# Routed attention into a mixture of experts on one core: the first head pair's loads, transposes, copies and idle products rearranged, and the score scale moved into the exponential

## The chip, the cores and the metric

The kernel runs on one core of a Trainium2 chip. The metric is device time in microseconds from the start to the end of one execution. Its engines are named as in the profile: PE is TensorE (PEld its weight loads), DVE is VectorE, ACT is ScalarE, POOL is GpSimd, SP is SyncE, which here only issues DMA. SP, ACT and POOL each have a queue in which they can issue DMA.

## The reference

Attention with 4 batches, 8 heads, 768 positions and head size 64, in which a query sees only the keys that fall to the same of 16 centroids; then a layer of 8 experts for the 3072 rows that come out. Cut to what matters:

```python
q_n, k_n, c_n = ...                        # rows divided by their norm
q_assign = np.argmax(np.einsum('bhsd,hcd->bhsc', q_n, c_n), axis=-1)
k_assign = np.argmax(np.einsum('bhsd,hcd->bhsc', k_n, c_n), axis=-1)
mask = q_assign[:, :, :, None] == k_assign[:, :, None, :]
scores = (1.0 / np.sqrt(D)) * np.matmul(q, k.transpose(0, 1, 3, 2))
scores = np.where(mask, scores, -1000000000.0)
attn = softmax(scores)                     # with 1e-9 added to the sum
x = (attn @ v)  as rows of 512: 3072 x 512
# experts: gate logits x @ w_gate, the best expert e of each row,
# y = gate * (relu(x @ w1[e]) @ w2[e])
```

## The kernel before

The attention goes through 16 pairs of heads (`g`). For each pair, q and k are loaded with positions on the 128 partitions, transposed on PE to `qk` (two heads of 64 on the partitions), multiplied with the normed centroids (`similar`), transposed back (`similar2`), and turned into one-hot rows (`assign`, `assign2`), which `put` transposes to `ohT`. A score tile is then the sum of two products in one PSUM tile: q times k, and one-hot times one-hot, scaled so that a pair of different clusters lies 2 to the 60th lower. Numbers at the left are the line numbers that the profile uses.

```python
# loads (L691, L696, L702, L704): q, k, v by SP, the small ones by ACT
702  nc.scalar.dma_start(out=csb, in_=centroids...)
704  nc.scalar.dma_start(out=wg_in, in_=moe_w_gate...)     # 512 pieces of 32 B
705  for f in (load_qk, load_v):
706      for g in range(2): f(g)                           # L691 q, k; L696 v
     # identity, then products of it with itself before there is data
711  ps = ps_m.tile([P, 512], F32, name="mps")             # pool ps_m: one buffer
712  for i in range(12):
713      nc.tensor.matmul(ps[:, 0:P], lhsT=ident, rhs=ident, start=True, stop=True)
     # POOL, in this order
718  nc.gpsimd.memset(wg, 0.0)                             # then one_row, L720, L721
724  nc.gpsimd.tensor_copy(wg[r, :, a, 0:E], wg_in[r])     # twice
727  nc.gpsimd.memset(ohs, 0.0)
731  nc.gpsimd.memset(t[:, 1, :], 0.0)                     # ohT, twice
     # norms of the centroids
737  nc.scalar.activation(csq, csb, AF.Square, accum_out=cs2)
739  nc.scalar.activation(cnrm, cs2, AF.Sqrt)
741  nc.scalar.activation(csq[:, 0:1], cnrm, AF.Exp)       # brings the table of Exp
     # L743 to L748: cinv from cnrm on DVE; L752: cn = csb * cinv, twice
754  nc.tensor.transpose(cps[:, 0:P], cn..., ident)        # cps is the mps buffer
757  nc.gpsimd.memset(cblk, 0.0)
760  nc.vector.tensor_copy(cblk[...], cview[...])          # twice

     def turn(g, piece):          # piece 0: 6 of q, 2 of k; piece 1: 4 of k
773      nc.tensor.transpose(ps[...], rows[g, "qk"[w]][:, j]..., ident)
         if piece == 0:
778          (g == 1)  nc.scalar.mul(flat[:, 0:S], ps[:, 0:S], D**-0.5)
780          (others)  nc.vector.tensor_scalar_mul(flat[:, 0:S], ps[:, 0:S], D**-0.5)
781          nc.scalar.copy(flat[:, S:1024], ps[:, S:1024])
         else:
783          nc.scalar.copy(flat[:, 1024 : 2 * S], ps[:, 0 : 2 * S - 1024])

790  # similar: four products, cblk with qk; L795: copy to simT on DVE
801  # similar2: three transposes; L803: copy to sim on ACT
809  nc.vector.tensor_reduce(mx, sim, axis=AX, op=ALU.max)               # assign
810  nc.vector.tensor_tensor(sim, sim, mx..., op=ALU.is_ge)
811  nc.gpsimd.tensor_tensor(sim, sim, first_c..., op=ALU.mult)
817  nc.vector.tensor_reduce(top, rank, axis=AX, op=ALU.max)             # assign2
821  nc.vector.tensor_tensor(ohs..., rank, top..., op=ALU.is_equal)      # twice
831  # put: six transposes of ohs; L836: copy to ohT[:, 0] on ACT
838  nc.vector.tensor_scalar(oh[..., 1, :], ps..., scalar1=BIG, scalar2=-BIG, ...)  # twice

858  # score(u): q times k, two products; L861: one-hots, two products
863  nc.scalar.activation(A[u], ps[:, :, 0:HS], AF.Exp)
866  # and L870: DVE adds A to the sums T; L878: attend, A times v
```

The order in which these stand on the engines is written out by hand. Turns of six score tiles follow each other; before turn 0 there are only preparations:

```python
if g == 0:
    at(-4, 0, turn, g, 0)
    at(-4, 1, turn, g, 1)
    at(-3, 0, similar, g)
    at(-3, 1, similar2, g)
elif g == 1:
    at(-2, 1, turn, g, 0)
    at(-2, 1, turn, g, 1)
    at(-1, 1, similar, g)
    at(0, 0, similar2, g)
...
at(n - 2, 0, assign, g)
at(n - 2, 0, assign2, g)
at(n - 1, 0, put, g)
```

The tiles `sps` (two PSUM banks each) have three buffers, which transposes, similarities and scores share.

Of the kernel before, what the change touches and what calls it, by code (L numbers as in the profile page):

```python
# [8 lines left out]
F32 = mybir.dt.float32  # L9
BF16 = mybir.dt.bfloat16  # L10
I32 = mybir.dt.int32
AX = mybir.AxisListType.X
AF = mybir.ActivationFunctionType
ALU = mybir.AluOpType
# [170 lines left out]
def kernel(  # L185
# [11 lines left out]
    nc = tc.nc  # L197
    B, H, S, D = q.shape
    C = centroids.shape[1]
    P = 128  # L200
    NQ = S // P
    HP = H // 2
    NG = B * HP
    HS = S // 2
    G = 4 * NQ
    N = B * S
    Dm = H * D
    E = moe_w_gate.shape[1]
    F = moe_w1.shape[2]
    DB = Dm // P  # L210
# [14 lines left out]
    consts = ctx.enter_context(tc.tile_pool(name="consts", bufs=1))  # L225
# [15 lines left out]
    ident = consts.tile([P, P], F32)  # L241
    ident_b = consts.tile([P, P], BF16)

    def iota(name, shape, pattern, base, mult):
        ti = consts.tile(shape, I32, name=name + "_i")
        tf = consts.tile(shape, F32, name=name)
        nc.gpsimd.iota(ti, pattern=pattern, base=base, channel_multiplier=mult)
        nc.gpsimd.tensor_copy(tf, ti)
        return tf
# [11 lines left out]
    ps_s = late.enter_context(tc.tile_pool(name="ps_s", bufs=3, space=PSUM))  # L261
    ps_o = late.enter_context(tc.tile_pool(name="ps_o", bufs=1, space=PSUM))
    ps_m = late.enter_context(tc.tile_pool(name="ps_m", bufs=1, space=PSUM))
# [4 lines left out]
    def wide():  # L268
        return pools["s"].tile([P, 2, 512], F32, name="sps")
# [248 lines left out]
    def cols_of(t, c0):  # L518
        return lambda j: t[:, c0 + j : c0 + j + 1]
# [126 lines left out]
    def indices(pool, ps, w, gi, si):  # L646
# [14 lines left out]
            n=[P] * n, rows=NF * P, e=e, gi=cols_of(g_idx1, sum(FT[:e])), si=cols_of(s_idx1, sum(FT[:e])), apart=True,  # L661
# [6 lines left out]
    with ExitStack() as actx:  # L668
# [11 lines left out]
        rows = {}  # L680
# [5 lines left out]
        def load_qk(g):  # L686
            b, hp = divmod(g, HP)
            for name, src in (("q", q), ("k", k)):
                t = rows[g, name] = ld.tile([P, NQ, 2, D], F32, name=name + "_in")
                for a in range(2):  # L690
                    nc.sync.dma_start(out=t[:, :, a, :], in_=src[b, 2 * hp + a].rearrange("(p j) d -> p j d", j=NQ))  # L691

        def load_v(g):
            b, hp = divmod(g, HP)
# [5 lines left out]

        csb = consts.tile([P, D], F32)
        nc.scalar.dma_start(out=csb, in_=centroids.rearrange("h c d -> (h c) d"))  # L702
        wg_in = consts.tile([P, DB, E], F32)
        nc.scalar.dma_start(out=wg_in, in_=moe_w_gate.rearrange("(a p) e -> p a e", p=P))  # L704
        for f in (load_qk, load_v):
            for g in range(2):
                f(g)
        make_identity(nc, ident)
        nc.vector.tensor_copy(ident_b, ident)

        ps = ps_m.tile([P, 512], F32, name="mps")
        for i in range(12):
            nc.tensor.matmul(ps[:, 0:P], lhsT=ident, rhs=ident, start=True, stop=True)
        first_c = iota("first_c", [P, C], [[-1, C]], C, 0)
        first_e = iota("first_e", [P, E], [[-1, E]], E, 0)

# [12 lines left out]
        for i in range(2):  # L729
            t = ohp.tile([P, 2, S], BF16, name=f"ohT{i}")  # L730
# [3 lines left out]

        csq = consts.tile([P, D], F32)
        cs2 = consts.tile([P, 1], F32)
        nc.scalar.activation(csq, csb, AF.Square, accum_out=cs2)
        cnrm = consts.tile([P, 1], F32)
        nc.scalar.activation(cnrm, cs2, AF.Sqrt)

# [9 lines left out]
        cn = consts.tile([P, 2, D], F32)  # L750
        for a in range(2):
            nc.vector.tensor_scalar(cn[:, a, :], csb, scalar1=cinv[:, 0:1], scalar2=None, op0=ALU.mult)  # L752
        cps = ps_m.tile([P, 512], F32, name="mps")
        nc.tensor.transpose(cps[:, 0:P], cn.rearrange("p a d -> p (a d)"), ident)

        cblk = consts.tile([P, HP, 2, C], F32)
        nc.gpsimd.memset(cblk, 0.0)
        cview = cps[:, 0:P].rearrange("p (g a c) -> p g a c", a=2, c=C)
        for a in range(2):
            nc.vector.tensor_copy(cblk[a * D : (a + 1) * D, :, a, :], cview[a * D : (a + 1) * D, :, a, :])  # L760


        qk, sims, ohT = {}, {}, {}

        def turn(g, piece):

            if piece == 0:
                qk[g] = qkp.tile([P, 2, S], F32, name="qk")
            ps = ps_s.tile([P, 2, 512], F32, name="sps").rearrange("p a c -> p (a c)")
            n = 4 if piece else 8  # L770
            for i in range(n):
                w, j = divmod(8 * piece + i, NQ)
                nc.tensor.transpose(ps[:, i * P : (i + 1) * P], rows[g, "qk"[w]][:, j].rearrange("p a d -> p (a d)"), ident)  # L773
            flat = qk[g].rearrange("p w s -> p (w s)")
            if piece == 0:

                if g == 1:
                    nc.scalar.mul(flat[:, 0:S], ps[:, 0:S], D**-0.5)
                else:
                    nc.vector.tensor_scalar_mul(flat[:, 0:S], ps[:, 0:S], D**-0.5)  # L780
                nc.scalar.copy(flat[:, S:1024], ps[:, S:1024])
            else:
                nc.scalar.copy(flat[:, 1024 : 2 * S], ps[:, 0 : 2 * S - 1024])

        def similar(g):

# [18 lines left out]
        def assign(g):  # L805

            sim = sims.pop(g)
            mx = asg.tile([P, G], F32, name="mx")
            nc.vector.tensor_reduce(mx, sim, axis=AX, op=ALU.max)
            nc.vector.tensor_tensor(sim, sim, mx.unsqueeze(2).to_broadcast([P, G, C]), op=ALU.is_ge)  # L810
            nc.gpsimd.tensor_tensor(sim, sim, first_c[:, None, :].to_broadcast([P, G, C]), op=ALU.mult)  # L811
            sims[g] = sim

        def assign2(g):
# [29 lines left out]
        A, T, O = {}, {}, {}  # L844
# [6 lines left out]
        def score(u):  # L851
            g, half, j = where(u)
            qs = slice(half * HS, (half + 1) * HS)
            ks = slice(j * P, (j + 1) * P)
            ps = ps_s.tile([P, 2, 512], F32, name="sps")
            for a in range(2):
                r = slice(a * D, (a + 1) * D)
                nc.tensor.matmul(ps[:, a, 0:HS], lhsT=qk[g][r, 1, ks], rhs=qk[g][r, 0, qs], start=True, stop=False)  # L858
            for a in range(2):
                r = slice(a * D, (a + 1) * D)  # L860
                nc.tensor.matmul(ps[:, a, 0:HS], lhsT=ohT[g][r, 1, ks], rhs=ohT[g][r, 0, qs], start=False, stop=True)  # L861
            A[u] = ap.tile([P, 2, HS], F32, name="A")
            nc.scalar.activation(A[u], ps[:, :, 0:HS], AF.Exp)  # L863
            if j == 1:
                T[g, half] = tp_.tile([P, 2, HS], F32, name="T", bufs=3)
                nc.vector.scalar_tensor_tensor(  # L866
                    T[g, half], in0=A[u - 1], scalar=1e-9 / P, in1=A[u], op0=ALU.add, op1=ALU.add
                )
            elif j > 1:
                nc.vector.tensor_tensor(T[g, half], T[g, half], A[u], op=ALU.add)  # L870
# [105 lines left out]
        def at(n, part, f, *a):  # L976
            jobs.setdefault((n, part), []).append((f, a))
# [7 lines left out]
        for g in range(NG):  # L985
            n = g * TG
            if g == 0:
                at(-4, 0, turn, g, 0)
                at(-4, 1, turn, g, 1)
                at(-3, 0, similar, g)  # L990
                at(-3, 1, similar2, g)
            elif g == 1:

                at(-2, 1, turn, g, 0)
                at(-2, 1, turn, g, 1)
                at(-1, 1, similar, g)
                at(0, 0, similar2, g)
            else:
                at(n - 3, 0, turn, g, 0)
                at(n - 3, 0, turn, g, 1)  # L1000
                at(n - 3, 1, similar, g)
                at(n - 2, 0, similar2, g)
# [3 lines that stand above are left out]
            at(n, 1, finish, g, 0)  # L1006
            at(n + 1, 1, finish, g, 1)
            if g < NG - 1:
                at(n + 2, 0, weigh, g)
                at(n + 2, 1, weigh2, g)  # L1010
                at(n + 2, 1, x_turn, g, 0)
                at(n + 3, 1, x_turn, g, 1)
                if g % HP == HP - 1:
                    at(n + 3, 0, gate, g // HP)
                    at(n + 3, 1, keep_rows, g // HP)
# [41 lines left out]
        n = (NG - HP) * TG  # L1057
# [11 lines left out]
        n = NG * TG  # L1069
# [34 lines left out]
    with tc.tile_pool(name="sm", bufs=1) as sm:  # L1104
# [20 lines left out]
        for part in parts:  # L1125
            n, over = part["n"], part["over"]
# [8 lines left out]
        for t0 in range(0, NT, TQ):  # L1135
# [10 lines left out]
            op=ALU.is_le,  # L1146
# [62 lines left out]
    g = groups[0]  # L1209
# [11 lines left out]
    for i, g in enumerate(groups):  # L1221

        if i + 1 < ng:
            n = groups[i + 1]
# [11 lines left out]
        n = groups[i + 2] if i + 2 < ng else None  # L1236
# [22 lines left out]
    with tc.If(more > 0):  # L1259
        nx = nc.values_load(xe[0:1, NX : NX + 1], min_val=0, max_val=NX)  # L1260
        general = nc.values_load(xe[0:1, NX + 1 : NX + 2], min_val=0, max_val=1)
        with tc.If(nx > XU):
            with ExitStack() as ectx:
# [3 lines left out]
                with tc.For_i(XU, nx, 1) as i:  # L1267
# [4 lines left out]
                    g = dict(  # L1272
                        n=[P], rows=N, w=(fetch1(ex, 0), fetch2(ex, 0)), gi=lambda j: gi[:, 0:1], si=lambda j: gi[:, 1:2], apart=False
                    )
# [36 lines left out]
```

## Time and profile before

| | before |
|---|---|
| time, median of 3 runs | 798.7 us (798.4 to 799.66) |
| span of the profiled run | 802.5 us |
| PE busy | 774.7 us, 97% |
| DVE busy | 484.0 us, 60% |
| ACT busy | 307.1 us, 38% |
| POOL busy | 110.1 us, 14% |
| moved by DMA | 81.75 MB |

A row of a busy time tells how long an engine had something to do, not whether somebody waited for it. A timeline row gives the start, the duration, the engine, the source line, what was written from what, and in square brackets how long the engine had stood idle and which instruction released it. A "q" behind an engine's name means its queue of DMA issues. In the timeline's counts a product of 4-byte numbers has two records. Matmuls' ends are modelled.

### The profile page before, as it was taken

Reading aid. Unit: us, or ns where it says so; the run is one execution under the profiler, and the core shown is the slowest. Engines: PE = TensorE matmul, PEld = TensorE weight load, DVE = VectorE, ACT = ScalarE, POOL = GpSimd, SP = SyncE. Lnnn points to the kernel's source line nnn. Section 1 sums busy time; section 2 is a strip of 40 time slices with the busy share of each in tenths; the row PEclk is TensorE's granted clock in tenths of the full one; section 3 lists DMA queues with packets and bytes.
Section 4 is the critical chain, followed back from the end, with each engine's and each line's share of the span. In section 5 each row is a group of like instructions: output and inputs, shape, how many; then the busy total and the mean of one; then the engine's idle time right before and its main releaser. Section 6 shows DMA issues by size and latency. Waiting matters only on the chain.

```text
span 802.5 us, 11975 instructions
## 1 busy us (share of the span) xinstructions
PE 774.7 (97%) x4813; PEld 505.5 (63%) x4813; DVE 484.0 (60%) x783; ACT 307.1 (38%) x479; POOL 110.1 (14%) x164
## 2 busy tenths in 40 slices
PE   6999999999999999999999899999999999999994
PEld 4545454545444544444575697989797969696861
DVE  3667667767667767787536336867484847471610
ACT  4554654554655554645510123232323232232120
POOL 2200000000000000022005423030303020101010
PEclk8999999999999999999999999999999999999998
DMA  9026420382231222201010347252525233241240
GB/s 217 2 60 238 91 60 24 117 269 60 60 98 45 57 60 60 99 2 40 1 70 37 102 150 267 105 171 105 191 105 175 105 111 154 67 178 57 99 148 17
DMA packets 76191, 81.75 MB, mean 102 GB/s; under 512 B 52831, under 2 KB 56927, under 8 KB 75616
## 3 DMA queue, kind: packets, MB, share of 16 engines
q1 hardware_dynamic: 70208, 60.82, 24.8%
q0 software_dynamic: 5248, 20.04, 7.6%
q8 instruction: 40, 0.66, 0.3%
q14 instruction: 23, 0.19, 0.1%
q10 hardware_dynamic: 672, 0.05, 0.1%
HBM read 68.26 MB, written 13.68 MB: 102 GB/s over the span
## 4 chain that ended last, share of the span: by engine, by line
PE 74%; issue 12%; DVE 7%; POOL 3%; ACT 2%; POOLq 0%; ACTq 0%; DVEq 0%
PE sps L858 15%; PE sps L475 14%; PE O L878 13%; PE sps L497 8%; PE sps L363 4%; PE sps L309 4%; PE sps L861 3%; DVE T L870 3%; PE mps L899 3%; PE sps L790 2%; PE sps L290 2%; PE sps L773 2%; POOL out_dram L327 1%; PE sps L944 1%; PE mps L912 1%
## 5 line engine op out<-in xcount | busy, mean ns | idle before, releaser
L863 ACT ACTIVATE A<-sps 128x768 f32<-128x768 f32 x192 | 153.2, 812 | 53.1 <-PE sps L861 51.9
L858 PE MATMUL sps<-qk 64*128 64x384 f32 x768 | 160.4, 496 | 0.1
L870 DVE TENSOR_TENSOR T<-T,A 128x768 f32<-128x768 f32 x128 | 122.7, 958 | 14.3 <-ACT lsT L905 0.5
L878 PE MATMUL O<-A,v_in 128*64 128x384 f32 x768 | 130.9, 490 | 0.0
L858 PEld LDWEIGHTS sps<-qk 64*128 64x128 f32 x768 | 66.9, 189 | 50.1 <-issue 42.5
L878 PEld LDWEIGHTS O<-A,v_in 128*64 128x64 f32 x768 | 52.3, 137 | 62.7 <-issue 62.6
L327 POOL DMA_INDIRECT out_dram<-zo,s_idx x34 | 33.0, 970 | 255.1 <-ACT zo L509 170.6
L363 PE MATMUL sps<-w,h_sb 128*128 128x512 f32 x144 | 63.6, 596 | 0.0
L861 PE MATMUL sps<-ohT 64*128 64x384 bf16 x384 | 63.6, 325 | 0.0
L866 DVE SCALAR_TENSOR_TENSOR T<-A 128x768 f32<-128x768 f32 x32 | 30.6, 958 | 49.3 <-ACT A L863 49.3
L475 PEld LDWEIGHTS sps<-xs,w1s 128*128 128x128 f32 x336 | 56.4, 190 | 5.7 <-issue 5.7
L475 PE MATMUL sps<-xs,w1s 128*128 128x208 f32 (+1 forms) x336 | 59.4, 333 | 0.6 <-DVE xs L385 0.6
L811 POOL TENSOR_TENSOR sim<-sim,first_c 128x384 f32<-128x384 f32 x16 | 16.0, 1000 | 263.8 <-DVE sim L810 263.8
L490 ACT ACTIVATE h_sb<-h_sb 128x832 f32<-128x832 f32 (+1 forms) x28 | 24.3, 867 | 69.8 <-DVE h_sb L431 69.8
L363 PEld LDWEIGHTS sps<-w,h_sb 128*128 128x128 f32 x144 | 26.7, 190 | 30.8 <-issue 30.6
L273 POOL DMA_INDIRECT xg<-x_rows,g_idx x34 | 36.6, 1078 | 38.5 <-ACT xgT L298 17.1
L497 PE MATMUL sps<-w2s,hs 128*128 128x256 f32 x168 | 38.6, 379 | 1.8 <-DVE w2s L385 1.8
L475 PE MATMUL sps<-xgT,w 128*128 128x208 f32 (+1 forms) x224 | 40.0, 331 | 0.0
L886 ACT COPY xT<-O 128x384 f32<-128x384 f32 x32 | 15.5, 484 | 61.6 <-PE O L878 61.6
L475 PEld LDWEIGHTS sps<-xgT,w 128*128 128x128 f32 x224 | 38.0, 190 | 0.0
L351 DVE TENSOR_TENSOR zc<-zc,sps 32x512 f32<-32x512 f32 x8 | 5.4, 675 | 53.6 <-ACT zc L350 53.6
L323 ACT ACTIVATE zo<-sps,gate 128x512 f32<-128x512 f32 x12 | 8.3, 688 | 73.9 <-PE sps L363 49.7
(246 smaller groups left out, 1063.0 us busy)
## 6 DMA issues: line engine op xcount, KB each, us to landing
w<-in_moe_w_dram SPq DMA_DIRECT2D x20, 2048.0 KB, 8.5
x_rows<-x POOLq DMA_DIRECT2D x4, 1548.0 KB
q_in<-in_q_dram SPq DMA_DIRECT2D x32, 192.0 KB, 4.5
k_in<-in_k_dram SPq DMA_DIRECT2D x32, 192.0 KB, 4.8
v_in<-in_v_dram SPq DMA_DIRECT2D x16, 384.0 KB, 3.3
xg<-x_rows,g_idx POOLq DMA_INDIRECT x34
out_dram<-zo,s_idx POOLq DMA_INDIRECT x34
csb<-in_centroids_dram ACTq DMA_DIRECT2D x1, 32.0 KB, 1.9
```

Source lines behind the costliest of these rows:

```text
L273: nc.gpsimd.indirect_dma_start(out=g["xg"][0:m, j, :], out_offset=None, in_=x_d[0 : g["rows"], :], in_offset=bass.IndirectOffsetOnAxis(ap= ...
L309: nc.tensor.matmul(o, lhsT=g["w"][0][:, c, fb * P : (fb + 1) * P], rhs=g["xT"][:, c, :cols], start=(c == 0), stop=(c == DB - 1),)
L327: ins = nc.gpsimd.indirect_dma_start(out=out[:, :], out_offset=bass.IndirectOffsetOnAxis(ap=g["si"](j)[0:m], axis=0), in_=zo[0:m], in_offs ...
L363: nc.tensor.matmul(zp, lhsT=g["h"][:, fb, j * P : (j + 1) * P], rhs=g["w"][1][:, fb, :], start=(fb == 0), stop=(fb == FB - 1),)
L475: nc.tensor.matmul(o, lhsT=a[:, c, f * P : (f + 1) * P], rhs=b[:, c, :], start=(c == 0), stop=(c == KH - 1),)
L497: nc.tensor.matmul(ps[:, 0, 0:DH], lhsT=a[:, f, :], rhs=b[:, f, :], start=(f == 0), stop=(f == FH - 1),)
L858: nc.tensor.matmul(ps[:, a, 0:HS], lhsT=qk[g][r, 1, ks], rhs=qk[g][r, 0, qs], start=True, stop=False)
L861: nc.tensor.matmul(ps[:, a, 0:HS], lhsT=ohT[g][r, 1, ks], rhs=ohT[g][r, 0, qs], start=False, stop=True)
L863: nc.scalar.activation(A[u], ps[:, :, 0:HS], AF.Exp)
L866: nc.vector.scalar_tensor_tensor(T[g, half], in0=A[u - 1], scalar=1e-9 / P, in1=A[u], op0=ALU.add, op1=ALU.add)
L870: nc.vector.tensor_tensor(T[g, half], T[g, half], A[u], op=ALU.add)
L878: nc.tensor.matmul(O[g, half][a * D : (a + 1) * D, 0:HS], lhsT=rows[g, "v"][:, a, j, :], rhs=a_[:, a, :], start=(j == 0), stop=(j == NQ - 1),)
```

## The change

The change concerns what happens before and while the first pair of heads is prepared, and, in two points, all pairs. Its parts:

- k of the first pair is issued by ACT's queue instead of SP's, so that q and k are issued side by side. The small load of `w_gate` goes from ahead of these loads to behind them.
- Squares and their sum for the centroids' norms move from ACT (with a table of its own) to DVE.
- The centroids' transpose and the copies to `cblk` go behind the first eight transposes of q and k, as a function `blocks`.
- A piece of `turn` now holds the same four positions of q and of k, so each fills one PSUM bank: DVE copies q's bank, ACT copies k's. The second piece (two positions of each) is copied by ACT.
- The scale 1/8 is no longer multiplied into q, but given to the exponential.
- The rank product of the first pair (L811) is done by DVE instead of POOL.
- The products of the identity with itself that keep PE busy ahead of the data are 8 instead of 12, and 3, 2 and 9 more stand in three gaps of the preparation.

```diff
-                    nc.sync.dma_start(out=t[:, :, a, :], in_=src[b, 2 * hp + a]...)
+                    (nc.scalar if g == 0 and name == "k" else nc.sync).dma_start(
+                        out=t[:, :, a, :], in_=src[b, 2 * hp + a]...)
 ...
         nc.scalar.dma_start(out=csb, in_=centroids...)
-        nc.scalar.dma_start(out=wg_in, in_=moe_w_gate...)
         for f in (load_qk, load_v):
             for g in range(2):
                 f(g)
+        nc.scalar.dma_start(out=wg_in, in_=moe_w_gate...)
 ...
+        def idle(ps, n):
+            for i in range(n):
+                nc.tensor.matmul(ps[:, 0:P], lhsT=ident, rhs=ident, start=True, stop=True)
+        def idle_of(n):
+            idle(ps_m.tile([P, 512], F32, name="mps"), n)
         ps = ps_m.tile([P, 512], F32, name="mps")
-        for i in range(12):
-            nc.tensor.matmul(ps[:, 0:P], lhsT=ident, rhs=ident, start=True, stop=True)
+        idle(ps, 8)
 ...
-        nc.scalar.activation(csq, csb, AF.Square, accum_out=cs2)
+        nc.vector.tensor_tensor(csq, csb, csb, op=ALU.mult)
+        nc.vector.reduce_sum(cs2, csq, axis=AX)
 ...     # cps, its transpose and the two copies to cblk: into a function
+        def blocks():
 ...
-            n = 4 if piece else 8
-            for i in range(n):
-                w, j = divmod(8 * piece + i, NQ)
-                nc.tensor.transpose(ps[...], rows[g, "qk"[w]][:, j]..., ident)
+            n = NQ - 4 if piece else 4
+            for i in range(2 * n):
+                w, j = divmod(i, n)
+                nc.tensor.transpose(ps[...], rows[g, "qk"[w]][:, 4 * piece + j]..., ident)
             if piece == 0:
-                if g == 1:
-                    nc.scalar.mul(flat[:, 0:S], ps[:, 0:S], D**-0.5)
-                else:
-                    nc.vector.tensor_scalar_mul(flat[:, 0:S], ps[:, 0:S], D**-0.5)
-                nc.scalar.copy(flat[:, S:1024], ps[:, S:1024])
+                nc.vector.tensor_copy(qk[g][:, 0, 0:512], ps[:, 0:512])
+                nc.scalar.copy(qk[g][:, 1, 0:512], ps[:, 512:1024])
             else:
-                nc.scalar.copy(flat[:, 1024 : 2 * S], ps[:, 0 : 2 * S - 1024])
+                nc.scalar.copy(qk[g][:, :, 512:S], ps[:, 0 : 2 * n * P]...)
 ...
-            nc.gpsimd.tensor_tensor(sim, sim, first_c..., op=ALU.mult)
+            (nc.gpsimd if g else nc.vector).tensor_tensor(sim, sim, first_c..., op=ALU.mult)
 ...
-            nc.scalar.activation(A[u], ps[:, :, 0:HS], AF.Exp)
+            nc.scalar.activation(A[u], ps[:, :, 0:HS], AF.Exp, scale=D**-0.5)
 ...
                 at(-4, 0, turn, g, 0)
+                at(-4, 0, blocks)
                 at(-4, 1, turn, g, 1)
+                at(-4, 1, idle_of, 3)
                 at(-3, 0, similar, g)
+                at(-3, 0, idle_of, 2)
                 at(-3, 1, similar2, g)
             elif g == 1:
                 at(-2, 1, turn, g, 0)
                 at(-2, 1, turn, g, 1)
+                at(-2, 1, idle_of, 9)
```

More of the change, by code (lines that the diff above doesn't have):

```diff
@@ L690, in load_qk @@
                 for a in range(2):
-                    nc.sync.dma_start(out=t[:, :, a, :], in_=src[b, 2 * hp + a].rearrange("(p j) d -> p j d", j=NQ))
+                    (nc.scalar if g == 0 and name == "k" else nc.sync).dma_start(
+                        out=t[:, :, a, :], in_=src[b, 2 * hp + a].rearrange("(p j) d -> p j d", j=NQ)
+                    )
         def load_v(g):
@@ L702 @@
         nc.scalar.dma_start(out=csb, in_=centroids.rearrange("h c d -> (h c) d"))
-        wg_in = consts.tile([P, DB, E], F32)
-        nc.scalar.dma_start(out=wg_in, in_=moe_w_gate.rearrange("(a p) e -> p a e", p=P))
         for f in (load_qk, load_v):
@@ L707 @@
                 f(g)
+        wg_in = consts.tile([P, DB, E], F32)
+        nc.scalar.dma_start(out=wg_in, in_=moe_w_gate.rearrange("(a p) e -> p a e", p=P))
         make_identity(nc, ident)
         nc.vector.tensor_copy(ident_b, ident)
+        def idle(ps, n):
[3 more added lines that the diff above has]
+            idle(ps_m.tile([P, 512], F32, name="mps"), n)
         ps = ps_m.tile([P, 512], F32, name="mps")
-        for i in range(12):
-            nc.tensor.matmul(ps[:, 0:P], lhsT=ident, rhs=ident, start=True, stop=True)
+        idle(ps, 8)
         first_c = iota("first_c", [P, C], [[-1, C]], C, 0)
@@ L752 @@
             nc.vector.tensor_scalar(cn[:, a, :], csb, scalar1=cinv[:, 0:1], scalar2=None, op0=ALU.mult)
-        cps = ps_m.tile([P, 512], F32, name="mps")
-        nc.tensor.transpose(cps[:, 0:P], cn.rearrange("p a d -> p (a d)"), ident)
         cblk = consts.tile([P, HP, 2, C], F32)
         nc.gpsimd.memset(cblk, 0.0)
-        cview = cps[:, 0:P].rearrange("p (g a c) -> p g a c", a=2, c=C)
-        for a in range(2):
-            nc.vector.tensor_copy(cblk[a * D : (a + 1) * D, :, a, :], cview[a * D : (a + 1) * D, :, a, :])
+        def blocks():
+            cps = ps_m.tile([P, 512], F32, name="mps")
+            nc.tensor.transpose(cps[:, 0:P], cn.rearrange("p a d -> p (a d)"), ident)
+            cview = cps[:, 0:P].rearrange("p (g a c) -> p g a c", a=2, c=C)
+            for a in range(2):
+                nc.vector.tensor_copy(cblk[a * D : (a + 1) * D, :, a, :], cview[a * D : (a + 1) * D, :, a, :])
         qk, sims, ohT = {}, {}, {}
@@ L768, in turn @@
                 qk[g] = qkp.tile([P, 2, S], F32, name="qk")
-            ps = ps_s.tile([P, 2, 512], F32, name="sps").rearrange("p a c -> p (a c)")
-            n = 4 if piece else 8
-            for i in range(n):
-                w, j = divmod(8 * piece + i, NQ)
-                nc.tensor.transpose(ps[:, i * P : (i + 1) * P], rows[g, "qk"[w]][:, j].rearrange("p a d -> p (a d)"), ident)
-            flat = qk[g].rearrange("p w s -> p (w s)")
-            if piece == 0:
-                if g == 1:
-                    nc.scalar.mul(flat[:, 0:S], ps[:, 0:S], D**-0.5)
-                else:
-                    nc.vector.tensor_scalar_mul(flat[:, 0:S], ps[:, 0:S], D**-0.5)
-                nc.scalar.copy(flat[:, S:1024], ps[:, S:1024])
+            n = NQ - 4 if piece else 4
+            ps = wide().rearrange("p a c -> p (a c)")
+            for i in range(2 * n):
+                w, j = divmod(i, n)
+                nc.tensor.transpose(ps[:, i * P : (i + 1) * P], rows[g, "qk"[w]][:, 4 * piece + j].rearrange("p a d -> p (a d)"), ident)
+            if piece == 0:
+                nc.vector.tensor_copy(qk[g][:, 0, 0:512], ps[:, 0:512])
+                nc.scalar.copy(qk[g][:, 1, 0:512], ps[:, 512:1024])
             else:
-                nc.scalar.copy(flat[:, 1024 : 2 * S], ps[:, 0 : 2 * S - 1024])
+                nc.scalar.copy(qk[g][:, :, 512:S], ps[:, 0 : 2 * n * P].rearrange("p (w s) -> p w s", w=2))
         def similar(g):
@@ L810, in assign @@
             nc.vector.tensor_tensor(sim, sim, mx.unsqueeze(2).to_broadcast([P, G, C]), op=ALU.is_ge)
-            nc.gpsimd.tensor_tensor(sim, sim, first_c[:, None, :].to_broadcast([P, G, C]), op=ALU.mult)
+            (nc.gpsimd if g else nc.vector).tensor_tensor(sim, sim, first_c[:, None, :].to_broadcast([P, G, C]), op=ALU.mult)
             sims[g] = sim
```

## The prediction

> **What bounds the kernel now.** I read the page first. It has TensorE (PE) busy for 774.7 of 802.5 us, 97% of the span, so an operation on another engine is worth nothing unless PE stands and waits for it. The two rows of forty slices (one slice is 20 us) tell where PE is not full: the first digit is 6, nearly all others are 9, and the granted clock is below full in the first slice too. The change works on that slice.
>
> ```profile
> PE   6999999999999999999999899999999999999994
> ...
> PEclk8999999999999999999999999999999999999998
> ```
>
> Then I read the timeline of the first 26 us for the order of events (columns: start, duration, engine, line, tiles; in square brackets what the engine waited for):
>
> ```profile
> 1.21 0.45 ACTq L704 DMA_DIRECT2D wg_in<-in_moe_w_gate_dram  x1
> 4.72 0.47 POOL L724 COPY wg<-wg_in 64x32 f32<-64x32 f32 x2 [2.20 <-DMA wg_in<-in_moe_w_gate_dram]
> 5.25 0.74 POOL L727 MEMSET oh<- 128x768 bf16 x1
> 5.92 1.50 POOL L731 MEMSET ohT<- 128x768 bf16 x2
> 7.37 0.20 POOL L757 MEMSET cblk<- 128x128 f32 x1
> 7.60 0.46 DVE L760 COPY cblk<-mps 64x64 f32<-64x64 f32 x2 [0.85 <-POOL cblk L757]
> 8.11 0.96 DVE L780 TENSOR_SCALAR qk<-sps 128x768 f32<-128x768 f32 x1
> 9.21 1.64 PE L790 MATMUL sps<-qk,cblk 128*32 128x384 f32 x8 [0.71 <-DVE qk L780]
> 13.84 0.99 POOL L811 TENSOR_TENSOR sim<-sim,first_c 128x384 f32<-128x384 f32 x1 [6.28 <-DVE sim L810]
> 16.14 0.82 PE L831 MATMUL sps<-ident_b,oh 128*128 128x128 bf16 x6 [2.77 <-DVE oh L821]
> 25.12 0.33 PE L861 MATMUL sps<-ohT 64*128 64x384 bf16 x2
> ```
>
> The rows form one chain: similarities of the first pair at 9.21, the transposes of its one-hot rows (L831) at 16.14, the last of the first six score tiles done at 25.12 + 0.33 = 25.45. From there PE is full. So **25.45 is the mark**: moving it moves the whole program, and nothing else in the change does. Note also what stands ahead of 9.21: GpSimd (POOL) waits for the small load wg_in until 4.72, then clears oh and the two ohT, and only then clears cblk, which VectorE (DVE) needs before it may write the centroid blocks. DVE lost 0.85 us to it already.
>
> Last, the clock by stretches (PE busy, clock, DMA share, GB/s):
>
> ```profile
> 8.55:11.95 3.40, 2.07 (x12) 1.00 1.14 299
> 11.95:15.35 3.40, 1.42 (x14) 1.00 1.33 235
> 15.35:18.75 3.40, 2.61 (x16) 0.54 1.23 265
> 18.75:22.15 3.40, 3.40 (x14) 0.50 0.52 84
> ```
>
> PE ran at half clock from about 15.6 to 22.2, after a stretch in which it was busy for 1.42 of 3.40 us.
>
> **What the Trainium skill says.** "TensorE: Matmul & The Clock Gate", part "What's actually happening": the clock is either half or full, and a free-running window of about 3.4 us decides it from how busy PE was. The trace agrees: 0.50 and 1.00 are the only levels, and the change back comes near 22.2 after a full stretch. That is the reason for the idle products. "DMA: Bandwidth & Descriptors", "Issuing engines are not separate DMA queues": two issuing engines share the same 16 DMA engines, only issue time is saved. "ScalarE: Activation LUTs", "What ACT_TABLE_LOAD costs": about 1283 ns a load; the trace has 1.28 us three times (1.69, 3.35, 4.87).
>
> **The change part by part.**
>
> 1. *Two queues.* In the old trace the four loads of the first pair were issued on one queue at 0.78, 1.51, 2.19 and 2.87 and landed 3.6, 3.9, 4.1 and 4.3 us later: 4.4, 5.4, 6.3, 7.2. About 0.9 us a load of 192 KB is 218 GB/s, the rate that the DMA view shows throughout: transfer sets the landings, not issue. With k on ScalarE's queue all four are in flight at once; the early slices, which had only 108 to 206 GB/s, fill up, so k lands perhaps 0.3 to 0.7 us sooner, but q, now sharing with k, later than 5.4.
>
> 2. *wg_in goes to the end of ScalarE's queue.* Issue starts after csb (ends 1.18) and two k loads of about 0.65 us each: 2.5. With its old 3.5 us to landing that is 6.0; behind 384 KB of k in the same queue I take **7.0** (between 6.0 and 7.8), against 4.7 now.
>
> 3. *What hangs on it.* POOL's order is unchanged, so from landing to a cleared cblk it is 7.57 - 4.72 = 2.85 us, and to the end of the two block copies on DVE 8.06 - 4.72 = 3.34 us: 7.0 + 3.34 = 10.35. Then the three idle products: they write the one mps buffer, which still holds the centroids' transpose, so they wait for the block copies and then stand ahead of the similarities. A product is two records; the warm ones at the end of L713 come eight in 0.9 us, 0.23 us a product, so 0.7 us. Similarities start at **11.1**, 1.9 us later than now.
>
> 4. *The other inputs are hidden behind that.* Loads by 7.0, eight transposes 1.0 (0.11 each and the tail), copy of 512 columns on DVE 0.96 - 256/0.96 ns = 0.69, then two copies on ScalarE (ACT) of 0.6 each: about 9.8. The two engines do not overlap here: in the built program's list of waits ACT's copy still waits for DVE's, as it did (ACT lost 2.7 us to DVE qk L780). So transposes ahead of the centroids' and the new banks gain nothing visible. The squares on DVE save a table load of 1.28 us, but the two k issues of 1.3 us now stand in front of ACT's first table load; the root comes at about 4.5 instead of 4.64. Zero.
>
> 5. *Similarities to one-hots.* Now 16.14 - 9.21 = 6.93 us. The eight records took 1.64 us because the second half waited for ACT; with all inputs ready later pairs take 0.85: -0.8. The rank product moves from POOL (0.99 plus a hand-over) to DVE, where its sister L810 takes 0.56: 13.84 to 14.87 becomes about 0.6, -0.45. Left 5.7. Beside it PE has the two idle products, three transposes, twelve of pair 1 (1.5 us) and nine idle products (2.1 us): done about 5.4 after the start if warm, so just in time. One-hot transposes at 11.1 + 5.7 = **16.8**, 0.65 later than now.
>
> 6. *Scores at full clock.* From L831 to the mark it is now 25.45 - 16.14 = 9.31 us. Warm: transposes until ACT can start 0.55 (0.86 cold), copy of ohT 0.80, two mask operations 1.14, hand-overs 0.3, last ohT product 0.33, then five tiles of 0.81 (the steady distance of L858) = 4.05: 7.15. That is -2.15.
>
> 7. *The scale in the exponential and the split copies in later pairs.* An Exp takes 0.81 us with or without it. In later pairs DVE's copy loses 0.27 us and ACT's gain 0.23, in series as before; PE waited for these copies about 4 us in all (2.4 for ACT L781, 1.6 for DVE qk). I put 0, within 0.5.
>
> Sum: +1.9 - 0.8 - 0.45 - 2.15 = -1.5 us at the mark.
>
> **Rivals.**
> (a) *The load of wg_in hides nothing* because two queues carry far more than one, and it lands near 6.0: similarities at 10.1, mark 2.5 us earlier, about 796.2. For it: between 3.5 and 4.0, with both queues active, 263 GB/s flowed. Against it: 217 GB/s in most other slices.
> (b) *The gap before the blocks makes the clock fall.* PE has nothing between the end of the transposes (about 8) and the idle products (10.4). In the stretch 8.55 to 11.95 it would be busy for about 1.5 us, like the 1.42 that cost the clock before. Then the nine idle products run at 0.43 us and hold up the one-hots by 1 to 2 us: gain 0, about 798.7. If also the first six tiles stay cold, 2.15 is not won and the kernel is up to 0.7 us slower. I give this 35%. The eight products at the start, which end near 4.9 instead of about 6.1, could also fail to raise the clock at all.
> (c) *Nothing waits for wg_in*, and the author's order pays in full: blocks at 8.5, similarities at 9.3, mark 3.3 us earlier, 795.4. The list of waits speaks against it.
>
> **Range and chances.** From 798.7: -1.5 by the sum, with a third of weight on (b), gives -1.3, 797.4 us. The best reading of (a) with some luck in later pairs is 795.8; the worst of (b) with half a microsecond of noise (runs before lie 798.4 to 799.66) is 799.3. The whole opening is 25 us and 2% is 16 us, so within 2% is all but certain.
>
> **What would show it right or wrong.** Right: POOL's copy of wg starts between 6 and 7.8; DVE's block copies have an idle time "POOL cblk" of over 1 us ahead of them; similarities start between 10 and 12, after the idle products; the rank product is 0.56 on DVE; clock 1.00 at the first scores; last of six tiles near 24. Wrong: wg_in landing before 5.5, PE waiting for ACT's copies of qk rather than for the blocks, a clock of 0.50 at the scores, or waits at L790 of later pairs that differ by over 1 us in sum. A time under 795 or over 800 would mean that something outside the opening moved.

## The result and the profile after

The changed kernel takes 803.06 us (802.52 to 803.37, 4 runs) against 799.18 us for the kernel before (798.4 to 800.13): ratio 1.0047, interval 1.003 to 1.0065. It is 3.9 us slower, where 1.3 us faster was predicted, and lies above the stated range of 795.8 to 799.3 us, though well within 2%.

First the timeline of the changed kernel, the rows that answer to those shown of before (start, duration, engine, line, what; in brackets the idle time and who ended it):

```profile
2.58 0.67 ACTq L710 DMA_DIRECT2D wg_in<-in_moe_w_gate_dram  x1
...
6.50 1.09 PE L785 MATMUL sps<-ident,q_in 128*128 128x128 f32 x4 [1.31 <-DMA q_in<-in_q_dram]
...
8.52 0.69 DVE L787 COPY qk<-sps 128x512 f32<-128x512 f32 x1 [2.14 <-PE sps L785]
...
8.70 0.47 POOL L733 COPY wg<-wg_in 64x32 f32<-64x32 f32 x2 [6.19 <-DMA wg_in<-in_moe_w_gate_dram]
...
9.25 0.58 ACT L788 COPY qk<-sps 128x512 f32<-128x512 f32 x1 [2.96 <-DVE qk L787]
...
11.26 0.20 POOL L764 MEMSET cblk<- 128x128 f32 x1
11.49 0.46 DVE L772 COPY cblk<-mps 64x64 f32<-64x64 f32 x2 [2.28 <-POOL cblk L764]
...
12.09 1.62 PE L716 MATMUL mps<-ident 128*128 128x128 f32 x6 [2.54 <-DVE cblk L772]
...
13.64 1.51 PE L797 MATMUL sps<-qk,cblk 128*32 128x384 f32 x8
...
20.54 0.51 PE L838 MATMUL sps<-ident_b,oh 128*128 128x128 bf16 x6
...
28.10 0.39 PE L868 MATMUL sps<-ohT 64*128 64x384 bf16 x2
```

Read down the starts. POOL waits 6.19 us for wg_in and gets it at 8.70, where it was 4.72. It clears oh and the two ohT, then cblk at 11.26. DVE has stood idle 2.28 us for that; the three idle products have waited for DVE's copies and take 1.62 us before the similarities may start at 13.64 (9.21 before). The mark, the end of the first six score tiles, is 28.10 + 0.39 = 28.49 us. Note also ACT's first copy of qk: 2.96 us idle, released by DVE's copy. The "two engines from two banks" work one after the other.

The opening of the kernel before is itself not fixed. A second profile of it, described below, has its mark at 23.87 us instead of 25.45 and no loss near 460 us, where the first one lost 3.4 us. Its 799.43 us lies in the middle of 28 timed runs of the kernel before (median 799.56), so the fair comparison is 28.49 against 23.87. From the mark to the end, the second profile of before needs 797.6 - 23.87 = 773.7 us, the changed kernel 801.6 - 28.49 = 773.1. Together 4.6 - 0.6 = 4.0 us: the 3.9 us that were timed. **All of the loss, and slightly more, is in the first 28 us.**

### The profile page after: what moved, and what is told of

It is laid out like the page before. It is cut to its first block, busy times and chain, and to the rows that moved or that the text cites. A ratio compares the mean times of both kernels' runs of the same rounds, so it can differ in the third digit from the quotient of the medians.

```text
span 801.6 us, 12011 instructions
## 1 busy us (share of the span) xinstructions
PE 776.4 (97%) x4833; PEld 508.3 (63%) x4833; DVE 481.7 (60%) x787; ACT 308.6 (39%) x475; POOL 109.3 (14%) x163
## 4 chain that ended last, share of the span: by engine, by line
PE 74%; issue 12%; DVE 6%; POOL 3%; ACT 2%; DMA 1%; ACTq 0%; POOLq 0%; DVEq 0%
PE sps L865 14%; PE sps L475 14%; PE O L885 13%; PE sps L497 8%; PE sps L363 4%; PE sps L309 4%; PE sps L868 3%; PE mps L906 3%; DVE T L877 3%; PE sps L797 2%; PE sps L290 2%; PE sps L785 1%; POOL out_dram L327 1%; PE sps L951 1%; ACT A L870 1%
```

## The experiments

The variants ran on several chips, whose level for the kernel before differs by 2 us (medians 799.5 to 801.6); only ratios, each to the kernel before on the same chip, are compared. On one of these chips (the variants cblk_pair1, after_one_queue, before_idle_rank and before_idle_rank_split) the profiles also show about 3.5 us lost near 460 us, as the first profile of before does, so these four spans are not set against the others'; their openings are.

### The kernel before, once more (before_again)

No edit.

> The kernel before, unchanged, for a second profile. In its first profile the first six score tiles ended at 25.45 us and some 3.6 us were lost near 460 us, and that execution was about 5 us over the median of the timed ones. Theory A (the changed kernel is slower because its opening is longer): the opening is the same again, mark near 25.4, and what was lost near 460 us is not there. Rival B (the clock's window falls differently in each execution): the half clock from 15.6 to 22.2 us is missing in this execution, and the mark lies near 23.3.

Measured: 799.43 us, mark 23.87. The half clock was there, but shorter. Windows of this second profile (PE busy, clock, DMA share, GB/s):

```profile
15.30:18.70 3.40, 2.77 (x18) 0.65 1.24 263
18.70:22.10 3.40, 3.40 (x26) 0.85 0.50 81
```

In the first profile the clock was at half from 15.6 until 22.4 (the prediction read 22.2; the column has 0.58 between 22.0 and 22.5); here it is at half from 16.3 to 19.7. Neither expectation held fully: the clock fell in both, but for 3.4 us in one and for 6.8, twice as long, in the other. The Trainium skill, "TensorE: Matmul & The Clock Gate", part "What's actually happening", calls the window free-running, and these two executions agree with it. My mark of 25.45 was the long one.

### wg_in issued ahead of k (after_wg_first)

```diff
+        wg_in = ...; nc.scalar.dma_start(out=wg_in, ...)
         for f in (load_qk, load_v): ...
-        wg_in = ...; nc.scalar.dma_start(out=wg_in, ...)
```

> The changed kernel with one thing undone: the load of wg_in is issued ahead of k's loads again. Theory A (wg_in's landing at 8.70 us holds up GpSimd's clearing of cblk, so the similarities start at 13.64): landing near 4.9, block copies right behind DVE's copy of qk at about 9.2, similarities near 11.1, mark (end of the first six score tiles) 2.5 us earlier than the changed kernel's 28.49, time about 800.5. Rival B (the cold TensorE clock costs it, the landing does not): similarities still later than 13 and the time within 0.5 us of 803.

Measured: ratio 1.0027 (1.0019 to 1.0035), mark 26.79, 1.7 us earlier. wg_in was there at 4.50, as expected, and a new wait took its place. Timeline of this variant:

```profile
4.50 0.47 POOL L733 COPY wg<-wg_in 64x32 f32<-64x32 f32 x2 [1.98 <-DMA wg_in<-in_moe_w_gate_dram]
...
7.14 0.20 POOL L764 MEMSET cblk<- 128x128 f32 x1
...
8.63 1.09 PE L785 MATMUL sps<-ident,k_in 128*128 128x128 f32 x4 [0.95 <-DMA k_in<-in_k_dram]
...
12.50 1.51 PE L797 MATMUL sps<-qk,cblk 128*32 128x384 f32 x8
```

cblk is cleared at 7.34, but PE now waits for k, whose transposes start at 8.63 instead of 7.40: k stands behind wg_in in ACT's queue, is issued half a microsecond later and landed near 8.5 us instead of 7.3. PE was still at half clock, so the similarities again took 1.51 us. The wait moved from wg_in to k, and less was won than expected.

### cblk cleared before POOL waits for wg_in (after_cblk_first)

```diff
+        cblk = consts.tile([P, HP, 2, C], F32)
+        nc.gpsimd.memset(cblk, 0.0)
         wg = consts.tile([P, DB, 2, 32], F32)
         nc.gpsimd.memset(wg, 0.0)
 ...
-        cblk = consts.tile([P, HP, 2, C], F32)
-        nc.gpsimd.memset(cblk, 0.0)
```

> The changed kernel with wg_in still late, but GpSimd clears cblk before it copies wg_in, so nothing of the opening waits for that landing but the clearing of oh and ohT. Theory A: same gain as with the load issued early, similarities near 11.1, time about 800.5; that would show that the landing matters through cblk alone. If instead it stays near 803, something else of the load (its packets beside k's) is what costs.

Measured: ratio 1.001 (1.0001 to 1.0019), mark 24.59, 3.9 us earlier than in the changed kernel. Timeline:

```profile
1.99 0.20 POOL L727 MEMSET cblk<- 128x128 f32 x1
...
8.30 0.47 POOL L736 COPY wg<-wg_in 64x32 f32<-64x32 f32 x2 [5.63 <-DMA wg_in<-in_moe_w_gate_dram]
...
9.39 0.45 DVE L773 COPY cblk<-mps 64x64 f32<-64x64 f32 x2
...
9.98 0.91 PE L716 MATMUL mps<-ident 128*128 128x128 f32 x6 [0.17 <-DVE cblk L773]
...
10.82 0.85 PE L798 MATMUL sps<-qk,cblk 128*32 128x384 f32 x8
```

wg_in is as late as ever (8.30) and hurts nobody: DVE's block copies follow its copy of qk at once. So the landing matters through cblk alone. And as PE has no gap of 2.5 us any more, the trace has full clock from 9.74 us instead of 17.65: the three idle products take 0.91 instead of 1.62 us and the similarities 0.85 instead of 1.51.

### Twelve idle products at the start (after_twelve)

```diff
-        idle(ps, 8)
+        idle(ps, 12)
```

> The changed kernel with 12 idle products at the start, as before, instead of 8. Theory A: the landing of wg_in still bounds the similarities, but with a warm clock the three idle products take 0.7 instead of 1.35 us, the similarities 0.85 instead of 1.5, and the transposes behind them half: 1.3 to 2 us earlier at the mark, time about 801.3. Rival B (cold clock is the whole cause): 3 us or more, time 800 or less. If the clock falls again in the gap ahead of the blocks: no gain.

Measured: ratio 1.0039 (1.0026 to 1.0052), which overlaps the changed kernel's; mark 27.51, 1.0 us earlier, of which 0.3 is an earlier landing of wg_in (8.42). The three idle products became warm (0.91 us), but the clock fell again directly behind them: similarities 1.51 as before. A warm start alone is worth little while PE then waits for the blocks (3.05 us here).

### No three idle products (after_no_three)

```diff
                 at(-4, 1, turn, g, 1)
-                at(-4, 1, idle_of, 3)
```

> The changed kernel without the three idle products that stand between the block copies and the similarities; the other idle products stay. In the changed kernel they ran from 12.09 to 13.71 us, cold, straight in the path. Theory A (they do not fill a gap, they lengthen the chain, since the single mps buffer makes them wait for the blocks first): similarities 1.5 us sooner, near 12.1, mark near 27.0, time 1.5 us nearer to the kernel before (ratio about 1.003 instead of 1.0047). Rival (they are what keeps the clock up for the stages behind): the similarities come sooner but the clock stays low longer, and the mark gains under 0.5 us.

Measured: ratio 1.0028 (1.0017 to 1.0039), similarities at 11.97, mark 26.82, 1.7 us earlier. The three products stood in the path and gave nothing for it: as they write the only mps buffer, they can't run while PE waits for the blocks, only after.

### Pair 1's copies back on ACT, cblk early (cblk_pair1)

```diff
-                nc.vector.tensor_copy(qk[g][:, 0, 0:512], ps[:, 0:512])
+                (nc.scalar.copy if g == 1 else nc.vector.tensor_copy)(qk[g][:, 0, 0:512], ps[:, 0:512])
```

(on top of the early cblk)

> The changed kernel with cblk cleared early (as in after_cblk_first) and, besides, pair 1's two bank copies both on ScalarE, as in the kernel before. In the changed kernel pair 1's first copy stands on VectorE behind the first pair's one-hots, so ScalarE's next two copies and then its copy of ohT come late: 22.07 where the one-hot transposes would have allowed about 21.1. Theory A (that order costs about 0.9 us): from the one-hot transposes to the mark 7.0 instead of 7.94 us, mark near 23.7, time 0.9 us under after_cblk_first's 800.0, about 799.1. Rival: the masks or the three score buffers bound the scores anyway, and the time stays at 800.

Measured: ratio 1.0004 (0.9991 to 1.0017), mark 23.77; from one-hot transposes to the mark 23.77 - 16.76 = 7.01 us, where it had been 24.59 - 16.65 = 7.94. The intervals of the two times overlap, so the clock time alone does not prove it; the timelines do. The changed kernel first, then this variant:

```profile
20.39 0.68 DVE L787 COPY qk<-sps 128x512 f32<-128x512 f32 x1
...
20.54 0.51 PE L838 MATMUL sps<-ident_b,oh 128*128 128x128 bf16 x6
21.11 0.58 ACT L788 COPY qk<-sps 128x512 f32<-128x512 f32 x1 [3.65 <-DVE qk L787]
21.59 0.59 ACT L790 COPY qk<-sps 128x512 f32<-128x512 f32 x1
...
22.07 0.82 ACT L843 COPY ohT<-sps 128x768 bf16<-128x768 bf16 x1
```

```profile
16.76 0.49 PE L839 MATMUL sps<-ident_b,oh 128*128 128x128 bf16 x6 [0.43 <-DVE oh L829]
...
17.29 0.80 ACT L844 COPY ohT<-sps 128x768 bf16<-128x768 bf16 x1 [1.81 <-PE sps L839]
```

In the changed kernel ACT stood idle 3.65 us, then had to do two copies for pair 1, and so copied ohT 1.5 us after the transposes began. Put back on ACT, the copies fall into its idle time, and ohT follows after 0.5 us.

### k on SP's queue again (after_one_queue)

```diff
-                    (nc.scalar if g == 0 and name == "k" else nc.sync).dma_start(
+                    nc.sync.dma_start(
```

> The changed kernel with k of the first pair on SP's queue again; wg_in, still last on ScalarE's queue, then follows the centroids directly. Theory A (the transfers share 16 engines, so two queues do not land k sooner, they land q later and push wg_in behind k): wg_in near 4.6, q near 5.3, k near 7.1; similarities near 10.5 and time like or under after_wg_first's 801.9, about 800.5. Rival (two queues do help and only the order of wg_in was wrong): k lands later than the 7.3 us it had with two queues, time above after_wg_first.

Measured: ratio 0.9992 (0.9977 to 1.0006), similarities at 9.86, mark 23.49. This one edit takes 5 us off the mark. Timeline of this variant:

```profile
4.46 0.51 POOL L733 COPY wg<-wg_in 64x32 f32<-64x32 f32 x2 [1.95 <-DMA wg_in<-in_moe_w_gate_dram]
...
5.38 1.09 PE L785 MATMUL sps<-ident,q_in 128*128 128x128 f32 x4 [0.19 <-DMA q_in<-in_q_dram]
...
9.86 0.85 PE L797 MATMUL sps<-qk,cblk 128*32 128x384 f32 x8
```

wg_in is there at 4.46 although it stands last: nothing large is ahead of it in its queue. The transposes of q start at 5.38 instead of 6.50, and the trace has full clock from 6.53 us, so the 5 us hold part of the cold clock as well. The landings come out of issue time and time to landing. With two queues q's two loads landed at 4.3 and 6.4 us and k's at 5.4 and 7.3; with one, in the second profile of before, at 4.2, 5.2, 6.1 and 7.0. With two queues k was complete no sooner, q came 1.2 us later, and wg_in 4 us later. The Trainium skill, "DMA: Bandwidth & Descriptors", part "Issuing engines are not separate DMA queues", says that loads issued by different engines run on the same 16 DMA engines and interleave; these landings agree with it.

### The three suspects undone together (three_undone)

k on one queue, cblk early, pair 1's copies on ACT; everything else of the change stays (edits as above).

> The changed kernel with the three suspects undone together and all else of the change kept: k back on SP's queue (so wg_in follows the centroids at once), cblk cleared early, pair 1's first copy back on ScalarE. Theory A (these three are the whole cause, and what is left of the change is the gain that was meant): after_one_queue's similarities at 9.9 and one-hot transposes at 15.5, and cblk_pair1's 7.0 us from there: mark near 22.5 against 28.49, rest of the program 773.1 us, ratio to the kernel before about 0.998. Rival (there is a further cost in the change, such as the copies by banks or the idle products): ratio 1.000 or more.

Measured: ratio 0.9987 (0.998 to 0.9993), mark 22.84, from the mark on 796.0 - 22.84 = 773.2 us. **With these three removed the change is a gain**, about a microsecond, near the 1.3 us that were predicted. There is no further large cost in it. A small one may be left: `before_idle_rank` below, the kernel before with two of the parts alone, has its mark at 22.31. Which part costs that half microsecond was not tested.

### Parts of the change in the kernel before

The nine idle products alone (before_idle):

```diff
                 at(-2, 1, turn, g, 1)
+                at(-2, 1, idle_of, 9)
```

> The kernel before with the nine idle products alone; the rank product stays on GpSimd. before_idle_rank measured 0.9979. Theory A (both parts pay): 0.45 us less gained, mark near 22.8, ratio about 0.9985. Rival (the idle products alone hold the clock and the rank product lies beside them): same as before_idle_rank.

Measured: ratio 0.9995 (0.9986 to 1.0003), mark 22.93. The mark is near where it was expected; the time is not clear of no difference. The spread does differ: 13 runs lie within 0.62 us (798.42 to 799.04) at a mean clock of 0.995 to 0.997. Of the 28 runs of before on that chip nine (798.27 to 798.94) have 0.995 or 0.996, and nineteen (799.28 to 800.67) have 0.993 or 0.994. So the nine products seem to bring the kernel to where its lucky runs were. They do not steady every kernel: `three_undone` has them too, with eight products at the start, and spreads over 2.5 us.

With the rank product on DVE besides (before_idle_rank):

```diff
-            nc.gpsimd.tensor_tensor(sim, sim, first_c..., op=ALU.mult)
+            (nc.gpsimd if g else nc.vector).tensor_tensor(sim, sim, first_c..., op=ALU.mult)
```

> The kernel before with two parts of the change alone: nine idle products between pair 1's transposes and the one-hot transposes, and the first pair's rank product on VectorE. Theory A (these parts are worth what the prediction said, and the rest of the change hid it): rank product 0.45 us, and the first scores at full clock, 0.8 to 2.1 us depending on where the clock's window falls; mark near 22.2 instead of 23.9 or 25.4, time about 797.9. Rival: idle products in the gap delay the one-hots or do not hold the clock, time 799 or more.

Measured: ratio 0.9979 (0.9969 to 0.9989), mark 22.31, 0.62 us before the former's. Both parts pay at the mark; in the time it is the two together that are clear of no difference.

With the scale in the exponential and the split copies in pairs 2 to 15 as well (before_idle_rank_split):

```diff
+            if g < 2: ...   # the old pieces
+            n = NQ - 4 if piece else 4        # else as in the changed kernel
-            nc.scalar.activation(A[u], ps[:, :, 0:HS], AF.Exp)
+            nc.scalar.activation(A[u], ps[:, :, 0:HS], AF.Exp, scale=D**-0.5)
```

> As before_idle_rank, with the scale in the exponential, and for pairs 2 to 15 the changed transposes and copies (512 columns by VectorE, the rest by ScalarE); pairs 0 and 1 keep the old pieces. From the mark to the end the changed kernel and its three variants took 773.1 to 773.2 us, the kernel before 773.7. Theory A: that half microsecond is the later pairs' shorter wait for copies, and comes here too: 0.6 us under before_idle_rank, about 797.3. Rival: it is noise of two executions, no difference.

Measured: ratio 0.9977 (0.9967 to 0.9987): no difference that the timing can tell. From the mark on it was 0.3 us shorter (776.7 against 777.0). Later pairs gain a few tenths at most.

### A version that beats both (q_then_k)

```diff
+            if g == 0:
+                # piece 0: q's six transposes, copied by DVE; piece 1: k's six, copied by ACT
+                ...
+                return
```

on top of the idle products, the rank product and the early cblk.

> before_idle_rank with two more steps for the first pair: one PSUM tile takes q's six transposes and the next k's six, so that VectorE copies q while ScalarE copies k and neither waits for the other; and cblk is cleared ahead of the wait for wg_in. In before_idle_rank ScalarE's copies waited for VectorE's and the second half of the similarities for ScalarE (8.93 to 10.57). Theory A: similarities from about 8.6 to 9.5, a microsecond earlier at their end, mark near 21.3, ratio about 0.9967. Rival: the landing of k or of pair 1's loads, or the nine idle products, then hold the one-hots, and nothing is gained over 0.9979.

Measured: ratio 0.9976 (0.9968 to 0.9985); 797.43 us (797.09 to 797.82), against 798.54 for the nine products alone on the same chip. Timeline:

```profile
7.65 0.96 DVE L780 TENSOR_SCALAR qk<-sps 128x768 f32<-128x768 f32 x1
8.30 0.80 ACT L782 COPY qk<-sps 128x768 f32<-128x768 f32 x1 [1.94 <-PE sps L778]
8.75 1.24 PE L804 MATMUL sps<-qk,cblk 128*32 128x384 f32 x8 [0.49 <-DVE qk L780]
```

With q and k in two tiles the two engines do overlap: ACT starts at 8.30, released by PE, while DVE works until 8.61. The similarities end at 9.99 instead of 10.57, the mark is 21.96. That is about half of the expected microsecond. At the mark only 0.35 us is left of it against `before_idle_rank` (22.31), and the ratios 0.9976 and 0.9979 can't be told apart: by the time, the rival's "nothing is gained" stands. What the start waits for now was not tested; in the trace the transposes of q (6.79) and of k (7.45) follow the centroids' transpose without a wait for a landing.

## Why the prediction was wrong

The chain was the right one and every link of it was seen: wg_in, then cblk, then the blocks, the idle products, the similarities, the one-hots, the scores. Four of its terms were too small, and the figure it started from was too large. Against -1.5 us at the mark stand +4.6: 4.5 of the 6.1 us between them are the terms of this table, 1.6 the starting figure.

| term | predicted us | measured us | miss |
|---|---|---|---|
| landing of wg_in | 7.0 | 8.70 | +1.7 |
| landing to the end of the block copies | 3.34 | 3.25 | -0.1 |
| block copies to similarities | 0.75 | 1.69 | +0.9 |
| similarities to one-hot transposes | 5.7 | 6.9 | +1.2 |
| one-hot transposes to the mark | 7.15 | 7.95 | +0.8 |
| mark | 23.95 | 28.49 | +4.5 |

**Landing of wg_in (step 2).** The step's range ended at 7.8. I had put it behind k, but let k land at 7.0. It took 6.1 us from issue, behind k in its queue and beside q's loads. Ahead of k (`after_wg_first`) it landed at 4.50, with k on the other queue (`after_one_queue`) at 4.46; `after_cblk_first` shows that cblk alone passes the delay on. What part its 512 small pieces have in the 6.1 us was not tested.

**Block copies to similarities, and on to the one-hots (steps 3 and 5): rival (b), and worse than I had it.** I took warm durations, those at full clock. The changed kernel was cold, at half clock, from its first product until 17.65 us. My mistake was to trust the clock column. Look at the column and at single products of the kernel before (min/median/max in ns), between 3.4 and 3.9 us and then between 5.6 and 6.3:

```profile
3.40:4.40 1.00, 1.00 (x7) 1.00 1.26 248
```

```profile
L713 PE MATMUL mps<-ident x4: 421/421/421, 3.1 to 3.7; 128*128 128x128 f32 x4
...
L713 PE MATMUL mps<-ident x6: 274/275/275, 5.4 to 5.9; 128*128 128x128 f32 x6
```

The column says 1.00 throughout; the products say that the clock came up only past 5 us. The first clock record of this trace begins at 5.36 us; ahead of it the column shows 1.00 whatever the clock is. In `after_twelve`, where the column does give 0.50 from 13 to 16 us, such records take 421 ns as well. The same in the changed kernel, whose first clock record begins at 17.65 us: the column, then the products at 12 and at 19 us:

```profile
11.90:15.30 3.40, 3.21 (x15) 1.00 1.31 245
...
L716 PE MATMUL mps<-ident x6: 421/421/550, 12.1 to 13.3; 128*128 128x128 f32 x6
...
L716 PE MATMUL mps<-ident x15: 275/275/275, 18.8 to 20.4; 128*128 128x128 f32 x15
```

Eight products are not too few in themselves. Here they end at 5.19 and PE then stands until q lands at 6.50; in `after_one_queue`, also with eight, q's transposes start at 5.38 and the clock is full from 6.53. Half clock costs 0.9 us in the three idle products, 0.66 in the similarities, 0.26 in the two idle products that delay the next transposes, and 0.3 in these transposes: together the two misses. `after_twelve` shows that a warm start does not help as long as the wait for the blocks lets the clock fall again; `after_cblk_first`, that without the wait even with eight products the clock is full by 10 us.

**One-hot transposes to the mark (step 6).** The clock was full there, as predicted. The 0.8 us are the copies of pair 1. Step 4 said rightly that the two copies are in series, and step 7 called the same copies free in later pairs, but I did not look at what DVE does just before pair 1's copy: it is busy with the first pair's one-hots. `cblk_pair1` measured 7.01 us, against my 7.15.

**The starting figure.** I read 25.45 us as the mark of the kernel before, from one execution. It was one with a long cold stretch, and a second had 23.87. From the one-hot transposes to the mark that second one needed 23.87 - 15.93 = 7.94 us and not 9.31: of the 2.15 us that step 6 meant to save, 1.4 were not there.

**The range.** It was narrower than my own rivals. A third of weight on (b), with its gain of 0, takes -1.5 to -1.0 and not to -1.3; and (b) at its worst, 0.7 us slower, with half a microsecond of noise is 799.9 and not 799.3. Even so the measured time lies beyond it. My sign that over 800 us something outside the opening must have moved was wrong too: the time is 803 us, and from the mark on the kernels differ by 0.6 us.

Right were: q later with two queues (step 1; that k would land 0.3 to 0.7 us sooner was not: 7.3 against 7.0 to 7.2), no gain from the squares on DVE (root at 4.57 against 4.64), the rank product (0.56 us on DVE), the exponential at 0.81 us with the scale in it, and later pairs within about half a microsecond (773.1 us from the mark on against 773.7). Rival (c) was rightly turned down: things did wait for wg_in. Rival (a), an early landing, was wrong by 2.7 us.

## What to carry to other kernels

Before a load is moved to the end of a queue, follow the engine that waits for it in order: here a 16 KB load held back the clearing of a tile that had nothing to do with it. Put what depends on no data ahead of the first wait, and see which buffer idle products write, or they wait for the very thing whose gap they should fill (a buffer of their own was not tried here). In an opening, take the clock from the durations of equal products and not from the clock column ahead of its first change, and profile it twice before taking a microsecond of it as given.

## What the runs showed of the hardware

- The clock column shows 1.00 in the first 5 us of the kernel before, while a record of a 128x128 product takes 421 ns instead of 275 and its weight load 333 instead of 192.
- The recorded changes of the clock lie multiples of 3.4 us apart. Cut there, in the first 30 us of the fourteen profiles, stretches at full clock in which PE was busy for 0.65, 0.80 and 1.19 us were followed by half clock; those with 1.95 us or more were not. Stretches at half clock (by the durations, ahead of the first record) with up to 2.87 us were followed by half clock again, those with 3.02 us or more by full clock. The changed kernel had 2.58, 2.11, 2.14 and 2.14 us in four stretches before the first full one.
- The 3.5 us near 460 us, in five profiles, are a wait of PE for ACT of 1.8 to 1.9 us (L309 for h_sb, in the layer of experts) and then half clock for 3.4 us. The nine other profiles, the changed kernel's among them, have neither. Why h_sb is late there in some executions stayed open.
